# Residual of an attention and mixing kernel by DMA transposes, with a fused relu and residual, outputs one period later and pooled copies on ScalarE

## The chip, the cores and the metric

One core of one Trainium2 chip. The metric is the device time of one execution in microseconds (us); lower is better. A profile is of one execution; its span is about 1.7 us shorter than the time. Besides the time, each execution leaves its span and its mean granted TensorE clock.

## The reference

Attention over 8 batches, 8 heads, 576 positions, 64 per head, in two parts, then a mixing stage whose output this change touches:

```python
x   = attention(q_mean4, k_mean4, v_mean4).repeat(4) + attention(q, k, v, |i-j| < 4)   # -> (8, 576, 512)
theta = x @ w_theta
y   = w_tok_r @ (x * cos(theta)) + w_tok_i @ (x * sin(theta))    # over the 576 positions
u   = x + y
out = u + maximum(u @ w_ch, 0)
```

## The kernel before

It is a software pipeline over batches. In one period it runs attention of batch b+1 (generator `a`), the theta stage of batch b (`m`) and the mixing and output of batch b-1 (`x`). A string of slots sets the order in which the generators give their pieces; a scheduler may still move instructions. In the first period there is nothing to mix yet, and the slots of `x` transpose the token weights (`wt`).

```python
PERIOD = ("m a m a a x m a x m a a x m a x m a "
          "a a x a a x a a x a a x a a x a x a a x a x a a x").split()
# 13 slots of x; of wt in the first period
```

u is made transposed (channels on partitions: `uT`), because that is how the last matmul needs it. The output needs u with positions on partitions, so each of five output chunks transposes it back on TensorE:

```python
for c in range(5):                       # ... chunk 4 has 64 positions and is folded
    psr = w1(...)                        # PSUM, 4 buffers shared by all w1 tiles
    psx = w1(..., BF16)
    # 4 matmuls   psr += uT[:, dc, chunk].T @ wch[:, dc, :]
    # 4 transposes psx = uT[:, dc, chunk].T
    nc.scalar.activation(out=rel, in_=psr, func=AF.Relu)
    nc.vector.tensor_tensor(out=osb, in0=rel, in1=psx, op=ALU.add)
    nc.sync.dma_start(out=out[b, ...], in_=osb)
```

Attention turns q and k on TensorE (`pstr`) into PSUM; ScalarE copies the full part to `qT`, `kT`, VectorE the mean of four, "pooled", to `qdT`, `kdT`. The local attention's exponentials `pm` (ScalarE) are masked by two affine selects each on GpSimd (POOL), then multiplied with v (`psloc`):

```python
nc.scalar.copy(out=dst, in_=src)             # qT, kT
nc.vector.tensor_copy(out=dstd, in_=srcd)    # pooled copies, 8 a batch
# ...
nc.scalar.activation(out=pm, in_=psS, func=AF.Exp, scale=SCL)
nc.gpsimd.affine_select(out=pm, ...); nc.gpsimd.affine_select(out=pm, ...)
```

The softmax here doesn't subtract the row's maximum and nothing guards it: scores larger than these inputs give would overflow.

## Time and profile before

| | |
|---|---|
| time | 334.36 us median of 3 runs (333.44 to 340.42; 340.42 is over 1.5% above the fastest and counts as slow) |
| span of the profiled run, mean granted TensorE clock | 334.4 us, 0.923 of full |
| TensorE busy | 88% of the span |
| from the start to the first theta matmul (the head) | 39.9 us |
| first period | 36.1 us |
| the six periods after it, together | 216.8 us |
| from the last theta stage to the end (the tail) | 41.6 us |

Periods are counted from the first theta matmul (`psth`) of one batch to that of the next. The page gives 40 equal slices of 8.4 us; one digit is a busy share in tenths, and PEclk the granted TensorE clock in tenths, 9 also for full speed:

```profile
PE   1688898999996899979997899889998999699994
PEclk9995589558999999979999999999998999979999
```

PE is busy for most of the program, and the clock is at half in the middle of the head and of the first period (the digits 5). The record of the clock starts only with its first change, here at 20.5 us; the digits 9 before it are no measurement. A table of windows, cut at the theta stages, gives the same by stage. Its columns are the stretch and its length in us, the busy time (and count) of PE, its weight loads, VectorE, ScalarE and POOL, then the granted clock, the DMA share and GB/s. First period, last full period, tail:

```profile
39.92:75.98 36.06, 33.34 (x322) 23.67 (x319) 23.46 (x52) 22.75 (x33) 20.30 (x23) 0.69 0.97 198
...
255.94:292.80 36.86, 33.56 (x338) 22.63 (x340) 21.21 (x51) 23.33 (x34) 10.27 (x10) 0.95 0.10 34
292.80:334.40 41.60, 36.72 (x278) 25.58 (x280) 17.33 (x35) 11.41 (x20) 0.00 (x0) 0.96 0.18 61
```

### The profile page before, as it was taken

To read this page: it belongs to the slowest core of one execution; us is meant where nothing else is said; L and a number is where in the kernel's file an instruction comes from. 1 tells how busy PE (TensorE), PEld (TensorE's weight loads), DVE (VectorE), ACT (ScalarE), POOL (GpSimd) and SP (SyncE) were. 2 spreads that over 40 slices of the span, in tenths; PEclk is the share of its full clock that TensorE was granted. 3 is DMA by queue.
4 is the path that set the end of the run, shared out by engine and by line. 5 is a ranking of instruction groups with operands and counts; after the bars stand their busy time and mean duration, and the time that the engine had idled before them with its cause. 6 is when DMAs were issued, how large, how long until landed. Compare 5 with 4: busy or idle time off the path is not lost.

```text
span 334.4 us, 7314 instructions
## 1 busy us (share of the span) xinstructions
PE 294.0 (88%) x2940; PEld 204.9 (61%) x2954; DVE 195.0 (58%) x441; ACT 186.0 (56%) x280; POOL 159.2 (48%) x186
## 2 busy tenths in 40 slices
PE   1688898999996899979997899889998999699994
PEld 1664685576664676557664666566755766467672
DVE  5426846594546764685439664766466544934533
ACT  1264289424874668628872787377855596333302
POOL 6977504893049524964477447815790008300000
PEclk9995589558999999979999999999998999979999
DMA  8999999959302289639917895477012000300303
GB/s 221 235 321 218 234 285 228 200 92 201 77 2 90 62 142 206 143 104 204 194 38 212 153 209 101 142 176 142 2 65 78 2 0 14 117 16 2 136 7 141
DMA packets 107826, 43.57 MB, mean 130 GB/s; under 512 B 97424, under 2 KB 101520, under 8 KB 107792
## 3 DMA queue, kind: packets, MB, share of 16 engines
q1 hardware_dynamic: 107792, 43.10, 58.6%
q8 instruction: 23, 0.38, 0.5%
q14 instruction: 11, 0.09, 0.1%
HBM read 33.65 MB, written 9.44 MB: 129 GB/s over the span
## 4 chain that ended last, share of the span: by engine, by line
PE 39%; ACT 17%; POOL 13%; issue 12%; DVE 10%; DMA 5%; SPq 3%; POOLq 0%; DVEq 0%; ACTq 0%
PE psu L553 13%; PE psth L528 9%; POOL pm L414 4%; POOL pm L416 3%; DVE tmp L486 3%; DMA q<-in_q_dram 3%; ACT pd L367 3%; POOL k_tm L143 3%; PE psr L573 3%; PE pstr L314 2%; ACT pm L401 2%; DVE osb L600 2%; PE pstr L304 2%; PE psnd L428 2%; DVE x L493 2%
## 5 line engine op out<-in xcount | busy, mean ns | idle before, releaser
L553 PE MATMUL psu<-WT,z 120*128 120x288 bf16 (+1 forms) x640 | 92.3, 291 | 0.0
L553 PEld LDWEIGHTS <-z 120*128 120x128 bf16 (+1 forms) x640 | 60.3, 99 | 18.4 <-issue 0.2
L414 POOL TENSOR_SCALAR_AFFINE_SELECT pm<-pm 128x1024 bf16<-128x1024 bf16 (+1 forms) x32 | 33.4, 1052 | 56.0 <-ACT pm L401 52.9
L401 ACT ACTIVATE pm<-psS 128x1024 bf16<-128x1024 f32 (+1 forms) x40 | 38.6, 982 | 20.7 <-PE psS L393 18.7
L528 PE MATMUL psth<-wth,xT 128*120 128x512 bf16 (+1 forms) x160 | 45.1, 405 | 4.7 <-DVE xT L518 3.8
L598 ACT ACTIVATE rel<-psr 128x512 f32<-128x512 f32 (+1 forms) x40 | 22.4, 559 | 48.1 <-PE psr L573 38.6
L143 POOL CAST q_tm<-q 96x1024 bf16<-96x1024 f32 x18 | 22.6, 1276 | 46.4 <-PE pstr L314 21.0
L535 ACT ACTIVATE cs<-psth,pihc 120x512 bf16<-120x512 f32 (+1 forms) x40 | 27.5, 688 | 29.9 <-PE psth L528 29.8
L537 DVE TENSOR_TENSOR z<-cs,x 120x1024 bf16<-120x1024 bf16 (+1 forms) x40 | 32.5, 813 | 18.6 <-ACT cs L536 18.5
L562 DVE TENSOR_TENSOR uT<-psu,xT 128x288 bf16<-128x288 f32 x64 | 26.8, 452 | 28.0 <-PE psu L553 28.0
L325 ACT CAST qT<-pstr 128x576 bf16<-128x576 f32 x32 | 20.2, 642 | 36.7 <-PE pstr L314 21.3
L600 DVE TENSOR_TENSOR osb<-rel,psx 128x512 f32<-128x512 f32 (+1 forms) x40 | 25.2, 631 | 21.5 <-ACT rel L598 21.5
L416 POOL TENSOR_SCALAR_AFFINE_SELECT pm<-pm 128x1024 bf16<-128x1024 bf16 (+1 forms) x32 | 33.7, 1059 | 0.8
L573 PE MATMUL psr<-wch,uT 128*128 128x512 bf16 x114 | 31.2, 379 | 1.4 <-issue 0.9
L477 PEld LDWEIGHTS <-pm 128*128 128x128 bf16 (+1 forms) x320 | 16.5, 112 | 21.9 <-POOL pm L416 13.8
L528 PEld LDWEIGHTS <-xT 128*120 128x120 bf16 (+1 forms) x160 | 20.5, 139 | 14.1 <-DVE xT L518 4.8
L518 DVE COPY xT<-xTps 128x480 bf16<-128x480 bf16 (+1 forms) x40 | 15.5, 389 | 23.3 <-PE xTps L513 23.2
L477 PE MATMUL psloc<-v_w,pm 128*128 128x65 bf16 (+1 forms) x320 | 19.5, 209 | 9.3 <-POOL pm L416 5.7
L486 DVE TENSOR_TENSOR tmp<-psloc,rl 120x512 bf16<-120x512 f32 (+1 forms) x40 | 26.5, 683 | 0.0
L493 DVE TENSOR_TENSOR x<-tmp,psup 120x512 bf16<-120x512 bf16 (+1 forms) x40 | 26.4, 680 | 0.0
L143 POOL CAST k_tm<-k 96x1024 bf16<-96x1024 f32 x18 | 19.6, 1114 | 12.9 <-PE pstr L314 12.0
L536 ACT ACTIVATE cs<-psth 120x512 bf16<-120x512 f32 (+1 forms) x40 | 23.6, 590 | 0.0
(87 smaller groups left out, 457.1 us busy)
## 6 DMA issues: line engine op xcount, KB each, us to landing
v<-in_v_dram SPq DMA_DIRECT2D x32, 256.0 KB, 5.4
out_dram<-osb SPq DMA_DIRECT2D x32, 256.0 KB, 2.0
q<-in_q_dram SPq DMA_DIRECT2D x36, 192.0 KB, 4.0
k<-in_k_dram SPq DMA_DIRECT2D x36, 192.0 KB, 4.7
q<-in_q_dram SPq DMA_DIRECT2D x8, 288.0 KB, 5.1
k<-in_k_dram SPq DMA_DIRECT2D x8, 288.0 KB, 6.1
v<-in_v_dram SPq DMA_DIRECT2D x8, 200.0 KB
wt<-in_moe_w_tok_r_dram SPq DMA_DIRECT2D x4, 288.0 KB
```

What stands on the lines that cost most here:

```text
L143: eng(out=dst[:, c:c + 2], in_=src.rearrange("p (c h d) -> p c h d", c=NTR, d=D)[:, c:c + 2])
L401: nc.scalar.activation(out=pv, in_=ps[0:kw].rearrange("p e (j w) -> p (e j) w", w=P)[:, :, 0:qn], func=AF.Exp, scale=SCL,)
L414: nc.gpsimd.affine_select(out=pv, in_=pv, compare_op=ALU.is_ge, fill=0.0, base=off, pattern=[[0, 8], [-1, qn]], channel_multiplier=1)
L416: nc.gpsimd.affine_select(out=pv, in_=pv, compare_op=ALU.is_ge, fill=0.0, base=6 - off, pattern=[[0, 8], [1, qn]], channel_multiplier=-1)
L477: nc.tensor.matmul(out=pv[0:qn, par, j, :], lhsT=pms[c][0:kw, 4 * par + j, 0:qn], rhs=v_w[0:kw, c, 2 * j + par, 0:65], start=(j == 0), sto ...
L486: nc.vector.tensor_tensor(out=tmp[0:cnt].rearrange("p (j e d) -> p e j d", e=2, j=4), in0=pv[0:cnt, :, :, 0:D], in1=rl[0:cnt].unsqueeze(3) ...
L493: nc.vector.tensor_tensor(out=x[0:cnt], in0=tmp[0:cnt], in1=up[0:cnt], op=ALU.add)
L528: nc.tensor.matmul(out=th[0:cnt, :], lhsT=xT[:, dc, QS[c]:QS[c] + cnt], rhs=wth[:, dc, :], start=(dc == 0), stop=(dc == 3),)
L537: nc.vector.tensor_tensor(out=z[0:cnt, c, :, :], in0=cs[0:cnt], in1=xt[c][0:cnt].unsqueeze(1).to_broadcast([cnt, 2, DM]), op=ALU.mult,)
L553: nc.tensor.matmul(out=pss[hf][:, 0:288], lhsT=z[0:QC[c], c, ri, P * dc:P * dc + P], rhs=WT[0:QC[c], ri, c, 288 * hf:288 * hf + 288], star ...
L573: nc.tensor.matmul(out=psr, lhsT=uT[:, dc, P * c:P * c + P], rhs=wch[:, dc, :], start=(dc == 0), stop=(dc == 3),)
L600: nc.vector.tensor_tensor(out=osb[:, 0:w], in0=rel[:, 0:w], in1=psx[:, 0:w], op=ALU.add)
```

## The change

The intent: take the 20 transposes a batch off PE, and the relu off ScalarE. uT is copied by two DMA transposes a batch into `uX` (positions on partitions), and one VectorE operation computes max(psr, 0) + uX. To give the transposes time, outputs come one period later, as a fourth generator `o`. ScalarE, freed of the relu, takes the pooled copies.

```diff
-    # relu on ScalarE, 4 (5) x 4 PE transposes, add on VectorE
-    nc.scalar.activation(out=rel[:, 0:w], in_=psr[:, 0:w], func=AF.Relu)
-    nc.vector.tensor_tensor(out=osb[:, 0:w], in0=rel[:, 0:w], in1=psx[:, 0:w], op=ALU.add)
+    # in mix, after every second dc:
+    nc.vector.tensor_copy(out=uT[:, dc - 1:dc + 1, S:640], in_=uT[:, dc - 1:dc + 1, 512:S])
+    nc.sync.dma_start_transpose(out=uX[:, dc - 1:dc + 1]..., in_=uT[:, dc - 1:dc + 1, :]...)
+    # in output, a period later:
+    nc.vector.scalar_tensor_tensor(out=osb, in0=psr, scalar=0.0, in1=uX[lo:hi, e:e + n, c, :],
+                                   op0=ALU.max, op1=ALU.add)
...
-                nc.vector.tensor_copy(out=dstd, in_=srcd)
+                (nc.vector.tensor_copy if b < WIDE else nc.scalar.copy)(out=dstd, in_=srcd)
...
-        "m a m a a x m a x m a a x m a x m a "
-        "a a x a a x a a x a a x a a x a x a a x a x a a x"
+        "m a m a a x m a x m a a x m a x m a x "
+        "a a o a a o a a o a a a a a o a x a a x a x a o"
...
-    for b in range(B + 1):
+    for b in range(B + 2):
+        run(a=attention(b + 1) ..., m=modulate(b) ...,
+            x=wt if b == 0 else mix(b - 1) if b <= B else None, o=output(b - 2) if b >= 2 else None)
...
-    t = moep.tile([P, S], FP32, tag=("osb", "rel")[ct % 2], bufs=3, ...)   # weight tiles, 6 buffers
+    t = moep.tile([P, S], FP32, tag="osb", bufs=4, ...)                    # 4 buffers
```

More of the change, by code (lines that the diff above doesn't have):

```diff
@@ L168, in staircase @@
                                     base=base, pattern=[[sgn * step, cols]], channel_multiplier=sgn * mul)
-    pw = moep.tile([TR, NTR, SD], BF16, tag="rel", bufs=3, name="pw")
+    pw = moep.tile([TR, NTR, SD], BF16, tag="pw", bufs=1, name="pw")
     nc.vector.memset(pw, 0.25)
@@ L241, in build_WT @@
     def build_WT():
-        w_tm = [moep.tile([P, 5, S], BF16, tag="uT", name=f"wtm{ri}") for ri in range(2)]
+        w_tm = [moep.tile([P, 5, S], BF16, tag="uX", name=f"wtm{ri}") for ri in range(2)]
         pieces = []
@@ L245, in build_WT @@
             for ct in range(5):
-                t = moep.tile([P, S], FP32, tag=("osb", "rel")[ct % 2], bufs=3, name=f"wt32_{ri}{ct}")
+                t = moep.tile([P, S], FP32, tag="osb", bufs=4, name=f"wt32_{ri}{ct}")
                 rows = OC[ct]
@@ L273, in build_WT @@
                 yield
+    uTs = [wpool.tile([P, 4, 640], BF16, name=f"uT{i}") for i in range(2)]
     xs = {}
@@ L500 @@
     state = {}
+    mixed = {}
     def modulate(b):
@@ L546, in mix @@
         xT, z = state.pop(b)
-        uT = moep.tile([P, 4, S], BF16, tag="uT", name=f"uT{b}")
+        uT = uTs[b % 2]
+        uX = moep.tile([P, 4, 5, P], BF16, tag="uX", name=f"uX{b}")
+        mixed[b] = (uT, uX)
         for dc in range(4):
@@ L565, in mix, with output @@
                 )
+            if dc % 2:
+                nc.vector.tensor_copy(out=uT[:, dc - 1:dc + 1, S:640], in_=uT[:, dc - 1:dc + 1, 512:S])
+                nc.sync.dma_start_transpose(
+                    out=uX[:, dc - 1:dc + 1].rearrange("p e c d -> p (e c) d"),
+                    in_=uT[:, dc - 1:dc + 1, :].rearrange("p e t -> p (e t)"),
+                )
             yield
+    def output(b):
+        uT, uX = mixed.pop(b)
         for c in range(5):
             psr = w1(f"psr{c}_{b}")
-            psx = w1(f"psx{c}_{b}", BF16)
+            osb = moep.tile([P, DM], FP32, tag="osb", bufs=4, name=f"osb{c}_{b}")
             if c < 4:
-                w = DM
                 for dc in range(4):
@@ L576, in mix @@
                     )
-                for dc in range(4):
-                    nc.tensor.transpose(
-                        out=psx[:, P * dc:P * dc + P], in_=uT[:, dc, P * c:P * c + P], identity=ident,
-                    )
+                parts = [(0, P, 0, 4)]
             else:
-                w = DM // 2
                 for dc in range(4):
@@ L586, in mix @@
                         nc.tensor.matmul(
-                            out=psr[64 * hf:64 * hf + 64, 0:w], lhsT=uT[:, dc, 512:576],
-                            rhs=wch[:, dc, w * hf:w * hf + w],
+                            out=psr[64 * hf:64 * hf + 64, 0:256], lhsT=uT[:, dc, 512:576],
+                            rhs=wch[:, dc, 256 * hf:256 * hf + 256],
                             start=(dc == 0), stop=(dc == 3),
                         )
-                for j in range(2):
-                    for hf in range(2):
-                        nc.tensor.transpose(
-                            out=psx[64 * hf:64 * hf + 64, P * j:P * j + P],
-                            in_=uT[:, 2 * hf + j, 512:576], identity=ident,
-                        )
@@ L597, in mix @@
-            rel = moep.tile([P, DM], FP32, tag="rel", bufs=3, name=f"rel{c}_{b}")
-            nc.scalar.activation(out=rel[:, 0:w], in_=psr[:, 0:w], func=AF.Relu)
-            osb = moep.tile([P, DM], FP32, tag="osb", bufs=3, name=f"osb{c}_{b}")
-            nc.vector.tensor_tensor(out=osb[:, 0:w], in0=rel[:, 0:w], in1=psx[:, 0:w], op=ALU.add)
-            if c < 4:
-                nc.sync.dma_start(out=out[b, P * c:P * c + P, :], in_=osb)
-            else:
-                for hf in range(2):
-                    nc.sync.dma_start(out=out[b, 512:576, w * hf:w * hf + w], in_=osb[64 * hf:64 * hf + 64, 0:w])
+                parts = [(0, 64, 0, 2), (64, 128, 2, 2)]
@@ L606, in mix @@
+            for lo, hi, e, n in parts:
+                nc.vector.scalar_tensor_tensor(
+                    out=osb[lo:hi, 0:P * n].rearrange("p (e d) -> p e d", d=P),
+                    in0=psr[lo:hi, 0:P * n].rearrange("p (e d) -> p e d", d=P),
+                    scalar=0.0, in1=uX[lo:hi, e:e + n, c, :], op0=ALU.max, op1=ALU.add,
+                )
+                nc.sync.dma_start(out=out[b, P * c:P * c + hi - lo, P * e:P * e + P * n], in_=osb[lo:hi, 0:P * n])
             yield
     PERIOD = (
-        "m a m a a x m a x m a a x m a x m a "
@@ L612, with run @@
-        "a a x a a x a a x a a x a a x a x a a x a x a a x"
+        "m a m a a x m a x m a a x m a x m a x "
+        "a a o a a o a a o a a a a a o a x a a x a x a o"
     ).split()
-    def run(a, m, x):
-        gens = {"a": a, "m": m, "x": x}
+    def run(**gens):
         for s in PERIOD:
-            g = gens[s]
-            if g is not None:
-                next(g, 0)
-        for s in ("m", "x", "a"):
+            if gens[s] is not None:
+                next(gens[s], 0)
+        for s in "mxoa":
@@ L627 @@
     next(wt)
-    for b in range(B + 1):
-        run(attention(b + 1) if b + 1 < B else None,
-            modulate(b) if b < B else None,
-            mix(b - 1) if b >= 1 else wt)
+    for b in range(B + 2):
+        run(a=attention(b + 1) if b + 1 < B else None,
+            m=modulate(b) if b < B else None,
+            x=wt if b == 0 else mix(b - 1) if b <= B else None,
+            o=output(b - 2) if b >= 2 else None)
 _INS = ['q', 'k', 'v', 'moe_w_theta', 'moe_w_tok_r', 'moe_w_tok_i', 'moe_w_ch']
```

## The prediction

> **What bounds the kernel now.** I read the page's busy shares first, then the table of windows cut at the first theta matmul (psth) of each batch, then the timeline of one period engine by engine, and last the tail. The program is a software pipeline: in one period it modulates batch b, mixes b-1 and runs attention on b+1.
>
> ```profile
> PE 294.0 (88%) x2940; PEld 204.9 (61%) x2954; DVE 195.0 (58%) x441; ACT 186.0 (56%) x280; POOL 159.2 (48%) x186
> ...
> core 0: us, PE busy (x) PEld busy (x) DVE busy (x) ACT busy (x) POOL busy (x), PEclk, DMA share, GB/s
> ...
> 149.69:185.11 35.42, 32.40 (x349) 22.11 (x351) 21.81 (x52) 24.02 (x37) 19.75 (x19) 0.99 0.79 158
> 185.11:220.75 35.64, 32.46 (x350) 22.37 (x352) 22.56 (x51) 23.41 (x36) 20.10 (x19) 1.00 0.78 158
> 220.75:255.94 35.19, 32.68 (x350) 22.45 (x352) 22.45 (x51) 23.41 (x36) 20.44 (x19) 1.00 0.37 88
> ```
>
> Periods are all 35.2 to 35.7 us, whether the DMA share is 0.79 or 0.37, so loads don't set them. PE looks 92% busy, but its ends are modelled. From start to start in the timeline, one psth or psr matmul costs 0.86/4 = 0.215 us of issue, one psu 1.47/12 = 0.1225, six pstr 0.32, eight psS or psloc 0.32. By that measure a period has about 30.6 us of PE issue and 4.9 us of gaps. PE is the fullest engine, not a saturated one. The rest is in the second half of the period:
>
> ```profile
> 238.83 1.02 ACT L401 ACTIVATE pm<-psS 128x1024 bf16<-128x1024 f32 x1
> ...
> 239.93 1.09 POOL L414 TENSOR_SCALAR_AFFINE_SELECT pm<-pm 128x1024 bf16<-128x1024 bf16 x1 [1.91 <-ACT pm L401]
> 241.09 1.09 POOL L416 TENSOR_SCALAR_AFFINE_SELECT pm<-pm 128x1024 bf16<-128x1024 bf16 x1
> 242.22 1.09 POOL L414 TENSOR_SCALAR_AFFINE_SELECT pm<-pm 128x1024 bf16<-128x1024 bf16 x1
> 243.38 1.09 POOL L416 TENSOR_SCALAR_AFFINE_SELECT pm<-pm 128x1024 bf16<-128x1024 bf16 x1
> 244.43 2.14 POOL L414 TENSOR_SCALAR_AFFINE_SELECT pm<-pm 128x1024 bf16<-128x1024 bf16 x2
> 246.52 2.14 POOL L416 TENSOR_SCALAR_AFFINE_SELECT pm<-pm 128x1024 bf16<-128x1024 bf16 x2
> 248.61 0.88 POOL L414 TENSOR_SCALAR_AFFINE_SELECT pm<-pm 100x768 bf16<-100x768 bf16 x1
> 249.56 0.88 POOL L416 TENSOR_SCALAR_AFFINE_SELECT pm<-pm 100x768 bf16<-100x768 bf16 x1
> ```
>
> From the first exp on, POOL masks without a gap for 10.5 us; the last local matmul waits for the last mask, and the next period starts 5.5 us later. POOL at 48% of the span is full in exactly this stretch. The end of the program is different, PE issues back to back:
>
> ```profile
> 324.66 1.03 PE L573 MATMUL psr<-wch,uT 128*128 128x512 bf16 x3
> 325.52 0.39 PE L578 MATMUL psx<-ident,uT 128*128 128x128 bf16 x4
> 325.75 1.03 PE L573 MATMUL psr<-wch,uT 128*128 128x512 bf16 x4
> 326.61 0.39 PE L578 MATMUL psx<-ident,uT 128*128 128x128 bf16 x4
> ```
>
> Here the start-to-start spacing tells what the removed transposes are worth: psx to the next psr is 325.75 - 325.52 = 0.23 us for four, though the group shows 0.39 us busy.
>
> [...] The trace has the first at 219 ns each, pipelined to 0.06; it holds no transposing DMA. [...] the 256 KB writes of this kernel land in 2.0 us, so I take 3 to 5 us from issue to landing. [...] the trace's residual adds take 684, so I leave the fused operation, still one pass with a PSUM input, at 0.69. [...] the trace's ScalarE copies of 128x144 take 279. [...]
>
> **The change, part by part.**
> 1. PE loses 4 x 4 + 4 transposes a batch: 5 x about 0.22 = 1.1 us a period, 8.8 us in all. This is the most that the PE part alone can give, 2.6%; the group's busy time (20 x 0.219 = 4.4 us) would promise four times that.
> 2. ACT loses the relu, 4 x 0.60 + 0.38 = 2.8 us a period, in the second half. It gains 8 pooled copies x 0.28 = 2.2 us in the first half, where from the theta stage to the first exp it already works about 15 of 18 us.
> 3. DVE loses the 8 pooled copies (8 x 0.30 = 2.4 us). The fused operation replaces the add one for one, except that the last chunk becomes two (+0.4), and two small copies of the tail columns come in (about 0.15 each, my guess). The residual no longer waits for the relu; PSUM is freed sooner.
> 4. The order changes. In the built program, PE has three output chunks (12 psr) but only 52 instead of 63 psu matmuls before the first scores: +12 x 0.215 - 11 x 0.1225 = +1.3 us, plus one or two pstr groups (0.3) that used to come before the theta stage. Hence the first exp comes about 1.4 us later. Going down ACT's new order with the trace's durations (five sine pairs at 1.28, copies at 0.64 + 0.28, table load 1.28, pooled exps 2.35) gives the same: first mask at about +20 to +20.6 after the theta start, against +19.2 now.
> 5. From there POOL's 10.5 us stand, and its built order has two or three casts of the next k and v inside this stretch (1.03 each; now zero to three), so +2.1 to 3.1. After the last mask the path to the next theta stage is shorter: no relu, no residual of this batch in the way, and the copy of x's first transposed chunk now stands ahead of the last tmp on DVE. I work it out as 0.6 (psloc) + 0.5 (psr, pstr) + 0.2 + 0.2 (transposes) + 0.4 (copy) + signals, 2.3 us against 3.5 to 5.5.
> 6. A middle period: 20.3 + 10.5 + 2.6 + 2.3 = 35.7, give or take one, against 35.5. So four middle periods give nothing. The second batch's period (37.95 now, four casts in the mask stretch) should lose about 2.5 us, having no output chunks and three casts; that with no casts (36.86 now) about 2.5 too.
> 7. The tail. Outputs of two batches follow the last mix instead of one, but their PE time has only moved there, and output 6 is used as filler. What is new: after the last mix come the second uT add (0.4), copy (0.15), the DMA transpose (3 to 5), then four fused operations and two half ones, 4 x 0.69 + 2 x 0.41 = 3.6 us. The last osb now ends 6 us after the last mix (324.7 to 330.7); then about 9 us. With about 3.9 us more psr after the last theta start and 1.5 us fewer PE transposes and gaps in it, the tail gets 4 to 6 us longer; I take 5.
> 8. The head: weight tiles have 4 buffers instead of 6, so SyncE stands at the fifth and the tenth weight load until POOL has cast the first of each half, and the loads of k for the third batch move from 45 to about 62 us. They are cast at 70 anyway. I put +0.5.
> Sum: -2.5 - 2.5 + 0.5 (middle periods, rounded) + 5 + 0.5 = +1 us, 335.4. My stage estimates lean cautious (the gaps of PE should shrink when its partners wait less), so I move to 333.
>
> **Rivals.**
> A: PE is the bound all through. Then 8.8 us go, and some of the 4.9 us gaps in each period with them: 334 - 9 - 6 x 1 + 5 = 324. For it: 92% in the windows. Against: the unbroken POOL stretch and the later first exp.
> B: the DMA transpose is slow[...]. Then SyncE's order (second transpose, then the next q loads) delays every load[...]. [...] Nothing in the profile before shows such a DMA, so I can't exclude it.
> C: ACT becomes the bound of the first half by the copies: the first exp another 1 us later in six periods, 340.
> D: POOL waits for k or v inside the mask stretch since q loads now stand behind the second transpose. The period from 113.95 had q loads at +4.6 us and k casts at +14.5 without harm, and I expect loads no later than that unless B holds.
>
> **Range and chances.** Between A (324) and the sum with C (341), with a tail of the range for B: 321 to 347, prediction 333. Faster by over 2% (under 327.7) needs periods below about 34 us with POOL's 10.5 us standing: 0.28. Slower by over 2% (above 341) needs B or C with D: 0.24. Within 2%: 0.48.
>
> **What would show it.** Right: no psx and no relu; period starts 35 to 36 us apart; first mask at +20 or later; POOL's masks with casts in between and no gaps; under 3 us from last mask to next theta start; transposes landing in 3 to 5 us; the last fused operation about 9 us after the last psu. Wrong in A's favour: periods near 33.5 and PE gaps gone. Wrong in B's: transposes of 8 us or more, SyncE standing still, q or k casts waiting for DMA. Wrong in C's: ACT without idle time before the first exp and PE waiting for its copies.

The forecast's sum came to +1 us, 335.4, and was shaded to 333. The 3 to 5 us for the transposing DMA, part of step 7's +5, is the estimate, above the 2.0 us in which the 256 KB writes of the kernel before land. In the paragraph of trace figures "the first" is a 128x128 transpose on TensorE. The 0.15 us for a small copy was a guess; the trace after has 0.18.

## The result and the profile after

350.16 us median of 4 runs (347.53 to 352.18) against 334.44 us for the kernel before on the same chip. The ratio is 1.047 (95% interval 1.040 to 1.055): slower. Ratios here compare fast runs of the same rounds and are not quite the ratio of the medians.

```profile
PE 292.7 (85%) x2794; PEld 196.9 (57%) x2794; DVE 199.7 (58%) x417; ACT 175.1 (51%) x288; POOL 154.6 (45%) x186
...
PE   0777995899979799879995999799968997799991
PEclk9995598556985999989999899999999999899996
```

146 PE matmul records fewer (2940 to 2794; 160 transposes were taken out, and the trace before lacks 14 of its 192 psr), yet PE's busy time fell by 1.3 us only. In the clock row the half-clock stretch of the first period reaches further (5, 5, 6 at the eighth to tenth digit, before 5, 5, 8), and a new one appears in the second period (8, 5 at the twelfth and thirteenth). By stage:

```profile
39.67:81.03 41.36, 35.84 (x341) 26.55 (x339) 25.10 (x52) 24.83 (x39) 23.54 (x27) 0.67 0.87 182
81.03:117.51 36.48, 31.41 (x285) 20.78 (x282) 16.21 (x36) 19.28 (x33) 16.87 (x18) 0.81 0.39 75
...
264.00:298.92 34.92, 30.05 (x307) 19.37 (x304) 20.28 (x45) 21.11 (x33) 10.20 (x10) 1.00 0.19 52
298.92:345.80 46.88, 39.12 (x264) 25.07 (x264) 21.97 (x47) 5.86 (x10) 0.00 (x0) 0.91 0.39 109
```

| stage, us | before | after | difference | predicted |
|---|---|---|---|---|
| head | 39.92 | 39.67 | -0.25 | in the next |
| first period | 36.06 | 41.36 | +5.30 | +0.5 |
| second period | 37.97 | 36.48 | -1.49 | -2.5 |
| four middle periods | 141.99 | 146.49 | +4.50 | +0.5 |
| last full period | 36.86 | 34.92 | -1.94 | -2.5 |
| tail | 41.60 | 46.88 | +5.28 | +5 |
| span | 334.40 | 345.80 | +11.40 | +1 |

This is the fastest of the four runs of the kernel after; the mean span of the four is 348.3 us.

**The first period.** The timeline of SyncE's issues shows a stand of 14 us, and that of PE the weight transposes (wps) at the period's end:

```profile
46.73 0.42 SPq L255 DMA_DIRECT2D w<-in_moe_w_ch_dram  x1
61.28 0.48 SPq L248 DMA_DIRECT2D wt<-in_moe_w_tok_i_dram  x1
61.82 5.54 SPq L94 DMA_DIRECT2D k<-in_k_dram  x6
```

```profile
70.48 1.67 PE L267 MATMUL wps<-ident,wtm 128*120 128x128 bf16 x10
...
78.78 0.85 PE L267 MATMUL wps<-ident,wtm 128*96 128x128 bf16 x5
...
81.03 1.91 PE L532 MATMUL psth<-wth,xT 128*120 128x512 bf16 x4
```

In the kernel before 20 of these 50 transposes ran at 52.9 to 55.9 us, between the pooled scores and at full clock; here all run from 62.7 us on and at half clock (ten in 1.67 us; at full clock, in run 15 below, ten take 1.11). The stand and the late transposes come together here but are not one cause: run 5 below has the old slots with four buffers, and SyncE stands there too (46.5 to 61.4 us), yet 20 transposes run at 52.4 to 55.4 us and the first period takes 37.5 us.

**The middle.** Two period starts of this same run, one after a sparse stretch and one after a denser one. Windows of 3.4 us, with the clock third from last:

```profile
186.60:190.00 3.40, 1.70 (x23) 1.10 (x23) 2.27 (x6) 0.00 (x0) 3.40 (x5) 1.00 0.00 0
190.00:193.40 3.40, 3.40 (x27) 2.44 (x25) 2.67 (x6) 2.92 (x5) 0.15 (x1) 0.55 0.51 96
...
223.20:226.60 3.40, 2.22 (x30) 1.54 (x29) 3.04 (x8) 0.28 (x1) 2.99 (x4) 1.00 0.00 0
226.60:230.00 3.40, 3.38 (x33) 2.66 (x34) 2.65 (x6) 3.37 (x6) 0.00 (x0) 1.00 0.69 136
```

And PE's timeline there:

```profile
188.66 0.55 PE L480 MATMUL psloc<-v_w,pm 100*96 100x65 bf16 x8 [1.70 <-POOL pm L419]
...
190.58 1.96 PE L532 MATMUL psth<-wth,xT 128*120 128x512 bf16 x4
...
226.62 1.07 PE L532 MATMUL psth<-wth,xT 128*120 128x512 bf16 x4 [0.18 <-DVE xT L522]
```

PE waits 1.70 us for the last mask, is busy for 1.70 of 3.40 us, and in the next 3.4 us its clock is half: the four theta matmuls take 1.96 instead of 1.07 us, at the start of the next period. (The lengths of two such periods are not compared here: some q transposes fall now before, now after the theta stage, which moves work between neighbours.) Taken in windows of 1 us over the whole trace, the clock is always 0.50 or 1.00 but for transitions, and its half-clock stretches last 3.4 us or multiples (3.4, 10.2, 17.1, 27.3), but for one that the end of the program cuts. In the profile of the kernel before they sum to 51 us, in that of the kernel after to 70. The full-clock stretches between them are whole multiples of 3.41 us too (13.7 to 105.8 us), so in both traces all changes of the clock lie on one grid of 3.41 us, the clock's own steps in what follows. The two windows shown above do not start with the clock's own steps; in those, PE is busy for 1.70 us from 186.9 to 190.3, and for 2.25 and 2.92 us from 221.0 to 224.4 and on to 227.8.

**The tail.** VectorE's timeline:

```profile
333.43 0.82 DVE L568 TENSOR_TENSOR uT<-psu,xT 128x288 bf16<-128x288 f32 x2 [1.63 <-PE psu L559]
...
334.50 0.18 DVE L573 COPY uT<-uT 128x128 bf16<-128x128 bf16 x1
...
338.79 2.48 DVE L603 SCALAR_TENSOR_TENSOR osb<-psr,uX 128x512 f32<-128x512 f32 x4 [3.65 <-DMA uX<-uT]
341.68 0.88 DVE L603 SCALAR_TENSOR_TENSOR osb<-psr,uX 64x256 f32<-64x256 f32 x2 [0.41 <-DMA out_dram<-osb]
```

From the last uT add to the last osb it takes 9.1 us (333.43 to 342.56); before, 6.0. 3.65 us of it is VectorE standing for the transposing DMA, which lands in 3.9 us at the median (3.4 to 4.5; SyncE takes 1.26 to 1.37 us to issue one, up to 3.27 among loads):

```profile
uX<-uT SPq DMA_TRANSPOSE x16, 3.9
```

### The profile page after: what moved, and what is told of

It reads as the page before. It is cut to its first block, busy times and chain, and to the rows that moved or that the text cites. A ratio compares the mean times of both kernels' runs of the same rounds, so it can differ in the third digit from the quotient of the medians.

```text
span 345.8 us, 7013 instructions
## 1 busy us (share of the span) xinstructions
PE 292.7 (85%) x2794; PEld 196.9 (57%) x2794; DVE 199.7 (58%) x417; ACT 175.1 (51%) x288; POOL 154.6 (45%) x186
## 4 chain that ended last, share of the span: by engine, by line
PE 49%; POOL 17%; ACT 13%; DVE 9%; issue 6%; DMA 4%; SPq 1%; DVEq 0%; ACTq 0%; POOLq 0%
PE psu L559 17%; PE psth L532 11%; POOL pm L417 8%; POOL pm L419 6%; PE pstr L317 5%; PE psr L587 3%; ACT pd L370 2%; ACT L370 2%; ACT vd L350 2%; DMA q<-in_q_dram 2%; ACT pm L404 2%; PE xTps L517 2%; PE pstr L307 2%; POOL k_tm L143 2%; DVE tmp L489 2%
## 5 line engine op out<-in xcount | busy, mean ns | idle before, releaser
L559 PE MATMUL psu<-WT,z 120*128 120x288 bf16 (+1 forms) x640 | 96.6, 294 | 0.8 <-DVE uT L568 0.4
L328 ACT CAST qT<-pstr 128x576 bf16<-128x576 f32 x32 | 20.7, 646 | 73.5 <-PE pstr L317 57.1
L541 DVE TENSOR_TENSOR z<-cs,x 120x1024 bf16<-120x1024 bf16 (+1 forms) x40 | 31.8, 794 | 20.0 <-ACT cs L540 19.8
L603 DVE SCALAR_TENSOR_TENSOR osb<-psr,uX 128x512 f32<-128x512 f32 (+1 forms) x48 | 28.6, 600 | 24.9 <-PE psr L587 20.5
L143 POOL CAST q_tm<-q 96x1024 bf16<-96x1024 f32 x18 | 20.2, 1126 | 45.7 <-DMA q<-in_q_dram 24.2
L587 PE MATMUL psr<-wch,uT 128*128 128x512 bf16 x128 | 32.6, 380 | 0.0
L480 PE MATMUL psloc<-v_w,pm 128*128 128x65 bf16 (+1 forms) x320 | 20.4, 212 | 14.2 <-POOL pm L419 12.0
L489 DVE TENSOR_TENSOR tmp<-psloc,rl 120x512 bf16<-120x512 f32 (+1 forms) x40 | 27.3, 684 | 0.3
L496 DVE TENSOR_TENSOR x<-tmp,psup 120x512 bf16<-120x512 bf16 (+1 forms) x40 | 26.6, 668 | 0.1
L143 POOL CAST k_tm<-k 96x1024 bf16<-96x1024 f32 x18 | 18.7, 1043 | 7.2 <-DMA k<-in_k_dram 4.0
L470 PE MATMUL psup<-xd,ru 72*128 72x512 bf16 (+1 forms) x48 | 20.1, 458 | 0.9 <-DVE x L496 0.8
```

The lines of the kernel that those rows point to most:

```text
L143: eng(out=dst[:, c:c + 2], in_=src.rearrange("p (c h d) -> p c h d", c=NTR, d=D)[:, c:c + 2])
L480: nc.tensor.matmul(out=pv[0:qn, par, j, :], lhsT=pms[c][0:kw, 4 * par + j, 0:qn], rhs=v_w[0:kw, c, 2 * j + par, 0:65], start=(j == 0), sto ...
L489: nc.vector.tensor_tensor(out=tmp[0:cnt].rearrange("p (j e d) -> p e j d", e=2, j=4), in0=pv[0:cnt, :, :, 0:D], in1=rl[0:cnt].unsqueeze(3) ...
L541: nc.vector.tensor_tensor(out=z[0:cnt, c, :, :], in0=cs[0:cnt], in1=xt[c][0:cnt].unsqueeze(1).to_broadcast([cnt, 2, DM]), op=ALU.mult,)
L559: nc.tensor.matmul(out=pss[hf][:, 0:288], lhsT=z[0:QC[c], c, ri, P * dc:P * dc + P], rhs=WT[0:QC[c], ri, c, 288 * hf:288 * hf + 288], star ...
L587: nc.tensor.matmul(out=psr, lhsT=uT[:, dc, P * c:P * c + P], rhs=wch[:, dc, :], start=(dc == 0), stop=(dc == 3),)
```

## The experiments

Theory at the start: the loss is the first period (weights drained late), the tail (DMA latency) and a middle set by POOL. Rivals: the transposing DMAs hold up the loads; the ScalarE copies delay the scores; the clock. Eighteen runs, each in 3 rounds beside the kernel before on the same chip. All runs of the changed kernels were fast except three of the fourth. "Half" is the time at half clock: 2 x (1 - mean clock) x span, averaged over the fast runs, without the time before the clock's record starts (about 20 us); the stages are those of the one profiled run, in us.

| run | median | before | head | first | six periods | tail | half |
|---|---|---|---|---|---|---|---|
| kernel before | | 334.44 | 39.92 | 36.06 | 216.82 | 41.60 | 48 |
| kernel after | 350.16 | 334.44 | 39.67 | 41.36 | 217.89 | 46.88 | 75 |
| 1 first period as before | 350.23 | 335.84 | 40.89 | 37.35 | 224.28 | 48.18 | 76 |
| 2 last residual on PE | 346.22 | 335.84 | 39.93 | 41.18 | 220.74 | 44.65 | 69 |
| 3 no transposes, zeroed tile | 346.97 | 335.84 | 43.68 | 40.67 | 216.42 | 43.53 | 49 (see text) |
| 4 pooled copies on VectorE | 353.12 | 335.84 | 39.95 | 39.38 | 219.77 | 46.90 | 67 (1 run) |
| 5 outputs not a period later | 362.44 | 334.80 | 40.32 | 37.54 | 238.04 | 44.50 | 89 |
| 6 all residuals on PE | 350.36 | 334.80 | 39.23 | 41.17 | 222.53 | 45.87 | 75 |
| 7 after, 4 fills | 346.70 | 334.80 | 39.75 | 39.13 | 220.78 | 45.24 | 41 |
| 8 before, 4 fills | 339.45 | 334.80 | 39.09 | 36.79 | 220.83 | 39.99 | 28 |
| 9 slots as before | 347.34 | 335.69 | 41.26 | 39.71 | 217.15 | 46.88 | 81 |
| 10 before, ScalarE copies | 342.45 | 335.69 | 40.06 | 38.09 | 219.92 | 41.63 | 61 |
| 11 run 1 with 4 fills | 344.56 | 335.69 | 40.50 | 37.01 | 219.88 | 45.21 | 40 |
| 12 runs 1 and 2, 2 fills | 343.17 | 335.69 | 39.76 | 36.59 | 219.48 | 44.47 | 41 |
| 13 order alone | 349.63 | 334.85 | 39.90 | 38.68 | 223.87 | 45.85 | 67 |
| 14 no transposes, clean | 348.26 | 334.85 | 40.16 | 41.20 | 220.44 | 43.50 | 75 |
| 15 run 10 with 2 fills | 330.77 | 334.85 | 38.94 | 36.56 | 212.78 | 39.92 | 28 |
| 16 before, 2 fills at the last group | 334.85 | 334.85 | 40.31 | 35.60 | 214.98 | 41.61 | 45 |
| 17 before, 2 fills | 333.03 | 334.98 | 39.76 | 36.04 | 215.35 | 39.95 | 28 |
| 18 run 15 with one-row fills | 343.04 | 334.98 | 39.82 | 41.74 | 218.42 | 39.92 | 52 |

**1. The first period as before** (e1_head6)

```diff
-        for s in PERIOD:
+        for s in PERIOD0 if gens["x"] is wt else PERIOD:     # PERIOD0: the old string
-    t = moep.tile([P, S], FP32, tag="osb", bufs=4, ...)
+    t = moep.tile([P, S], FP32, tag=("osb", "wtb")[ct % 2], bufs=(4, 2)[ct % 2], ...)
```

> The kernel after, with the first period as before: the weight builder gets its 13 early slots again (the old slot string for that period alone) and six weight buffers instead of four. Head theory (the first period is 5.5 us longer because the 20 weight transposes ran at its end, at half the TensorE clock, after a load that waited for POOL's cast): the first period falls from 41.4 to 36-37 us, the whole from 350 to about 345. Rival (a disturbance that the transposing DMAs or the later outputs cause): there is neither in the first period, so it predicts nothing here, and the first period stays near 41.

The first period fell to 37.35 us as the theory had it. The whole did not move: 350.23. In the profiles (the slowest of this kernel's four runs against the fastest of the kernel after's) the periods after it took 6.4 us more, with more of them at half clock. So the slots and buffers together are behind the first period (run 5 parts them: it is the slots), but a gain there did not reach the end. That made the clock the main suspect.

**2. The last batch's residual on PE** (e2_tail)

```diff
-            if dc % 2:
+            if dc % 2 and not (b == B - 1):
+            pe = b == B - 1      # then 20 PE transposes, ACT relu, DVE add as in the kernel before
```

> The kernel after, with only the last batch's residual by 20 PE transposes, ACT relu and DVE add, as before; all other batches keep their DMA transposes. Tail theory (5.3 us of the loss: the last uT, its copy, a transposing DMA of about 4 us, then fused operations at 0.69 us each): the last stretch falls from 46.9 to 42-43 us, the whole from 350 to about 346. Rival (the tail is longer because two batches' outputs follow the last mix, whatever way the residual takes): it stays at 46 or more.

346.22, and the tail 44.65: 2.2 of the tail's 5.3 us are the transposing DMA and what follows it, the other 3 stay. By count these are the further output that now follows the last theta stage: 16 psr matmuls of 512 columns (0.215 us each) and 8 of 256 (0.46 us for all, from 329.10 to 329.56 us in the kernel before) are 3.9 us, less the 20 transposes that are saved there (1.1 us).

**3. and 14. No transposing DMAs** (e3_notranspose, e14_notranspose_clean)

```diff
-        uX = moep.tile([P, 4, 5, P], BF16, tag="uX", name=f"uX{b}")
+        uX = uX0                                              # run 3: one tile of zeros
+        uX = uT.rearrange("p e (c d) -> p e c d", d=P)        # run 14: the untransposed uT
-                nc.sync.dma_start_transpose(...)
```

> Wrong on purpose: the kernel after without its 16 transposing DMAs; the residual is read from one constant tile of zeros, everything else (small copies, fused operation, order) stays. Mask-stretch theory (the middle periods are set by when POOL's mask stretch starts and by the casts in it): the six middle periods stay within 0.5 us of the kernel after (about 36.5 on average) and only the tail loses 3-4 us; the whole about 346. Rival, contention (the transposing DMAs hold up the queue, so q, k and v come late and POOL waits): the middle periods fall by 1-2 us each and the whole to about 338.

> Wrong on purpose: the kernel after without its transposing DMAs; the fused operation reads the untransposed uT where it read the transposed copy, so there is no zeroing any more. If the transposing DMAs cost nothing but the tail: head 39.7, middle periods as in the kernel after, tail 43.5, the whole 346-347. If they also delay the loads and so bring casts into the mask stretch and the clock down: middle periods near 35, half-clock time 50-60, the whole 340-343.

Both give wrong results. Run 3 has an artefact: its head is 43.7 instead of 39.7 us. The zeroing delays the first PE instruction by 0.9 us only; but PE stays slow through the whole head (the first four theta matmuls take 1.91 us at 43.68), and the clock's record starts at 45.8 us instead of 19.6. So its 49 us leave out more than the others' and are not to be compared. Run 14 has none and gives 348.26, a tail of 43.50 instead of 46.88, a first period and half-clock time as in the kernel after. It misses its 346 to 347: the whole fell by 1.9 us only, as the six periods took 2.5 us more in its profile. So the transposing DMAs cost the tail about 3.4 us, and taking them out makes nothing else shorter; contention is out.

**4. Pooled copies on VectorE again** (e4_dvecopies)

```diff
-                (nc.vector.tensor_copy if b < WIDE else nc.scalar.copy)(out=dstd, in_=srcd)
+                nc.vector.tensor_copy(out=dstd, in_=srcd)
```

> The kernel after, with the pooled copies on VectorE again. If the copies on ScalarE delay the first exp (8 x 0.28 us in ScalarE's filled first half, the rival C of the prediction): the first mask comes 1 to 1.5 us sooner after the theta start in each middle period, periods fall by about 1 us, the whole to 343-345. If the three early output chunks on PE delay the scores instead: the first mask stays at about +20.7 and the whole within 1.5 us of 350.

Three of four runs counted as slow (over 1.5% above the fastest, 347.77); it is no gain. From the third period on the first masks came at +20.5 to +22.1 us: no better. The first period of the one fast run is 39.38 us against 41.36, though.

**5. Outputs in the same period** (e5_samelag)

```diff
+    def both(b):
+        yield from mix(b)
+        yield from output(b)
-            x=wt if b == 0 else mix(b - 1) ..., o=output(b - 2) if b >= 2 else None)
+            x=wt if b == 0 else both(b - 1), o=None)          # and the old slot string
```

> The kernel after with its order taken back: outputs follow their own mix in the same period, in the slot string of the kernel before; the DMA transposes, the fused operation and the copies on ScalarE stay. Order theory (the loss comes from the outputs moved one period later: a first period that drains the weight transposes at its end, a mask stretch left without dense matmuls so that the TensorE clock is halved more often, a tail with two batches' outputs): half-clock time, 69 us in the kernel after, returns to about 50 as before, first period 36, tail 44-45, the whole 333-338. Rival (the transposing DMAs, the fused operation or the copies cost the time themselves): it stays at 345 or more.

362.44: the expectation of the order theory fell flat. With no period between, VectorE stands for the transposes in the middle of the program too. The waits of this run:

```profile
DVE osb L607 <- DMA uX<-uT: 11.6, 5, 3.6
```

The columns are us in all, times, longest. 11.6 us of direct waits are not the whole of 28 us; in the second period (47.8 us) GpSimd waited 9.3 us for one exponential, and half-clock time rose to 89 us. How these waits chain up was not followed further. The delay of a period is needed by the DMA transposes, so they cannot be tried without it.

**6. and 13. The order without DMA transposes** (e6_pe_residual, e13_order_alone)

```diff
+            pe = True            # run 6: every residual by PE transposes, relu, add
+                nc.vector.tensor_copy(out=dstd, in_=srcd)     # run 13: and the pooled copies on VectorE
```

> The kernel after with its order and its ScalarE copies, but every residual by 20 PE transposes, ACT relu and DVE add; no DMA transposes. Order theory: first period still 41 us, half-clock time still 65-75 us, tail 44-45 (as in the run with only the last batch so), the whole 345-350. Rival (DMA transposes delay the loads and with them the periods): the middle periods return to 35.5 and the whole to about 340.

> The order alone: outputs one period later in the new slots, four weight buffers; but residuals by PE transposes, ACT relu, DVE add, and pooled copies on VectorE, as before. If the order is what thins PE in the mask stretch: half-clock time 70 us or more, first period 40-41, tail 45, the whole 346-350. If the ScalarE copies were needed for the loss (350.4 with both, 342.5 with the copies alone): about 341-343.

350.36 and 349.63 (the first period of run 13 is 38.7 us, not 40 to 41). Outputs one period later in the new slots cost 15 us by themselves; with the ScalarE copies on top it is the same, and with the DMA transposes on top (the kernel after, 350.16) again the same. What the DMA transposes and the fused operation save on PE and ScalarE does not show. So the order is enough for a loss of this size. It is not the same loss, stage by stage: the six periods of run 13 are 6 us longer than those of the kernel after, its first period 2.7 us shorter. "Order" here is the later outputs, the new slots and the four weight buffers together.

**7. and 8. Useless work** (e7_fill_after, e8_fill_before)

```diff
             ps = w2(f"psloc{c}_{b}")
+            for i in range(4 if b > 0 else 0):
+                nc.tensor.matmul(out=ps[:, 1, :], lhsT=wth[:, 0, 0:P], rhs=wth[:, 0, :], start=True, stop=True)
```

> The kernel after with useless work added: four 128x512 matmuls (4 x 0.215 us) before each psloc group of the batches from the second on, into the PSUM tile that psloc then overwrites; 140 matmuls, about 30 us of PE time in all. Clock theory (PE too sparse in the mask stretch, so the clock is halved in steps of 3.4 us there and at the start of the next period): half-clock time falls from 69 us to about 45, first masks come at +19.5 instead of +20.9 after the theta start, and the whole falls to 342-347 although PE has more to do. Rival (PE is the bound): the whole rises by up to 30 us, to 365-380; neither: 350.

> The kernel before with the same useless matmuls. Clock theory: its half-clock windows at 58-79, 146-151 and 256-260 us (27 us in all) mostly go, in the first period above all; 330-336 against 335, since its second halves are denser and the fill then also costs some time. Rival (PE bound): 350 or more.

140 more matmuls of 128x512 made the kernel after 3.5 us faster (ratio 1.037, 1.031 to 1.043, against 1.047, 1.040 to 1.055), and half-clock time fell from 75 to 41 us. PE is not the bound; its clock matters. (From the third period on first masks came at +19.85 to +20.5, not quite +19.5.) The kernel before lost 4.7 us by the same fill (ratio 1.014): it was dense already. The pair also shows what is left where the clock is nearly even (in the six periods, one stretch of 10 us at half clock against none): six periods 220.78 against 220.83, first period +2.3, tail +5.2. The prediction's claim is about the four middle periods: these take 148.4 against 147.3 us, 1.1 us more, with no half clock in either. But the fill itself makes the kernel before's middle 5.3 us longer, so this is not a test of the bare kernels.

**9. The old slots for the mixing** (e9_old_slots)

```diff
-        "m a m a a x m a x m a a x m a x m a x a a o a a o a a o a a a a a o a x a a x a x a o"
+        "m a m a a x m a x m a a x m a x m a a a x a a x a a x a a x a a o a o a a o a o a a o"
```

> The kernel after with another slot string: the mixing keeps all its slots of the kernel before (the scheduler builds 60 to 63 psu and no psr ahead of the scores, as before), and the output chunks, still one period later, stand in the mask stretch, where they stood before. Clock theory: PE is dense in the mask stretch again, half-clock time falls from 69 us to 50-60, middle periods to 35-35.5, the whole to 340-345 (the tail stays at 46, the first period at 38-41). Rival (the middle lost its time to the later scores of PE's new order): the first masks come at +19.2 whatever the clock does, and the periods fall likewise; told apart by the half-clock windows at the periods' starts. If neither: 350.

347.34, and half-clock time did not fall (81 us): the expectation fails. Moving the output chunks back into the mask stretch does not by itself keep the clock; with all the mixing ahead of the scores the stretch has 4 psr a chunk and still no transposes.

**10. One part alone: the ScalarE copies** (e10_before_act_copies)

```diff
-                nc.vector.tensor_copy(out=dstd, in_=srcd)                  # in the kernel before
+                (nc.vector.tensor_copy if b < WIDE else nc.scalar.copy)(out=dstd, in_=srcd)
```

> The kernel before with one part of the change alone: the eight pooled copies on ScalarE instead of VectorE. Rival C of the prediction (ScalarE bounds the first half): first masks 1 us or more later than +19.2 and the whole 340-342. If ScalarE has room between the sines: first masks within 0.4 us of +19.2, the whole 333-337.

342.45 (ratio 1.021, 1.014 to 1.027), the size of rival C. But its reason is wrong: the first masks came at +18.7 in the last three periods, sooner than +19.2, and these periods took 34.4 to 35.4 us. What grew are the first four, by 8.0 us together (153.2 against 145.2). The scheduler now puts all four q transposes ahead of the theta stage, where PE waits for ScalarE's copies, at half clock. PE's timeline at the end of the first period:

```profile
73.50 0.26 PE L314 MATMUL pstr<-ip,q_tm 96*128 96x120 bf16 x1 [0.36 <-ACT qdT L326]
...
78.09 0.26 PE L314 MATMUL pstr<-ip,k_tm 96*128 96x120 bf16 x1 [0.71 <-ACT qdT L326]
78.15 1.91 PE L528 MATMUL psth<-wth,xT 128*120 128x512 bf16 x4
```

**11. and 12. Causes taken away together** (e11_head_fill, e12_all_three)

```diff
# 11: edits of runs 1 and 7.   12: edits of runs 1 and 2, and the fill with range(2 ...)
```

> The kernel after with the first period of run one (old slots, six weight buffers) and the useless matmuls of the fill run together. If the 4 us that the old first period gained were lost again to the clock, then with the clock held they stay: 342-343 against 346.7 for the fill alone, first period 36-37. Rival (the weights' transposes only move, and the loads set the sum of the first periods): 346-347.

> The kernel after with the old first period, the last batch's residual by PE transposes, and half the fill (two useless matmuls before each psloc group): the three causes taken away together. If they are the whole of the loss and add up: first period 36-37, periods 35-36, tail 42-44, half-clock time about 45, the whole 335-339, level with the kernel before. If something else costs the time: above 342.

Run 11: 344.56 against 346.70 for the fill alone. With the clock held, 2.1 of the first period's gain stay, half of what was expected. Run 12 misses: 343.17 instead of 335 to 339. The tail is still 2.9 us longer than before and the periods 2.7 us; with half the fill the clock still fell twice in the two periods after the first, whose first half no fill reaches. The three causes do not add up to the whole. The amount of half clock is not all that is left, either: it is 41 us here, less than the 48 of the kernel before, and the run is still 7.5 us slower.

**15. and 17. The fill where the order is the old one** (e15_act_copies_fill, e17_before_fill2)

```diff
# 15: run 10 and the fill with range(2 ...)      17: the kernel before and the fill with range(2 ...)
```

> The kernel before with the ScalarE copies and two useless matmuls ahead of each psloc group. Its undisturbed periods were 34.4 to 35.4 us, but 58 us ran at half clock. If holding the clock is all that it lacks: half-clock time 35-40, periods 35-36 throughout, the whole 332-336 against 342.5 without the fill. If the copies cost time by themselves: 339 or more.

> The kernel before with two useless matmuls ahead of each psloc group, the copies still on VectorE. If the ScalarE copies are worth something once the clock is held: 334-336, 4 us above the same fill with the copies on ScalarE (330.8). If the fill alone made that gain: 330-332.

Run 15 is faster than both kernels: 330.77, ratio 0.988 (0.979 to 0.996), outputs correct; at the 2% that a verdict asks for it stays unclear. The same ScalarE copies that cost 7 us alone no longer cost time with the fill: run 15 is 2.3 us below run 17 (333.03, ratio 0.994, 0.991 to 0.998). That gain is less than the 4 us expected and not secure, as the two come from different chips and the intervals overlap.

**16. Very little fill** (e16_before_fill_last)

```diff
+            for i in range(2 if b > 0 and c == 4 else 0):     # in the kernel before
```

> The kernel before with only two useless matmuls a period, ahead of the last psloc group. Clock theory: the three half-clock windows at the starts of periods (10 us, worth about 0.35 us each us by the slope among runs of one kernel) go for 0.2 us a period: 332-334 against 335. If two are too few: 335-336.

334.85, ratio 0.997 (0.991 to 1.004): too few. Half-clock time fell by 4 us only.

**18. The same order, fills that hardly work** (e18_one_row_fill)

```diff
-    nc.tensor.matmul(out=ps[:, 1, :],   lhsT=wth[:, 0, 0:P],   rhs=wth[:, 0, :],   start=True, stop=True)
+    nc.tensor.matmul(out=ps[0:1, 1, :], lhsT=wth[0:1, 0, 0:1], rhs=wth[0:1, 0, :], start=True, stop=True)
```

> The kernel of the run with ScalarE copies and fill, instruction for instruction in the same order on every engine, but each useless matmul multiplies one row by one column of weights (still 512 wide), so PE is occupied as long and hardly works. If the other order made the gain, or if the clock follows PE's occupied time: 331 and 28 us at half clock, as there. If the clock follows the work done in the array: half-clock time 55-60 and 340-343, and then the order is not the cause.

A fill makes the scheduler place some other groups differently, so runs 7 to 17 alone leave open whether the clock or the order made the gain. Run 18 has the instructions of run 15 in the same order on every engine; only the fills use one row and one column of the array. 343.04 against 330.77, half-clock time 52 against 28. PE's timeline and the windows of run 15, first:

```profile
64.22 1.04 PE L475 MATMUL psloc<-wth 128*128 128x512 bf16 x2
```

```profile
66.00:70.00 4.00, 3.79 (x36) 2.19 (x37) 3.52 (x8) 0.00 (x0) 4.00 (x6) 0.78 1.21 197
70.00:74.00 4.00, 3.53 (x46) 2.80 (x45) 3.96 (x10) 2.20 (x6) 3.65 (x5) 1.00 0.49 110
...
78.00:82.00 4.00, 4.00 (x37) 2.91 (x34) 2.74 (x6) 2.23 (x5) 0.00 (x0) 1.00 0.93 193
```

and run 18:

```profile
64.57 1.01 PE L475 MATMUL psloc<-wth 1*1 1x512 bf16 x2
```

```profile
66.00:70.00 4.00, 4.00 (x28) 1.58 (x26) 2.98 (x8) 0.00 (x0) 3.93 (x7) 0.50 1.21 199
70.00:74.00 4.00, 4.00 (x26) 1.80 (x25) 2.36 (x7) 0.00 (x0) 4.00 (x5) 0.50 0.37 68
...
78.00:82.00 4.00, 3.29 (x29) 2.73 (x27) 1.59 (x4) 2.17 (x5) 1.34 (x2) 0.50 1.30 217
```

The fills themselves take as long in both (two in 1.04 and 1.01 us); around each pair PE loses about 0.18 us more with one row, as the gaps between starts show. With the array filled the clock is back at 1.00 from about 68 us; with one row it stays at 0.50 to the end of the first period, though PE is busy 4.00 of 4.00 us. Order does not make these 12 us. Most of them go with the clock: in the profiles 11.7 us, of which 8.4 lie in the first two periods, where run 18 has most of its extra half clock, but 1.7 in the last four full periods, at full clock in both, and 0.9 in the head, ahead of any fill. In this pair the clock goes with the work done in the array (28 us at half clock with it filled, 52 with one row), not with PE's occupied time.

**A rule that the traces give.** Which work the clock follows can be counted in the 20 traces, the two kernels' and the runs'. Cut each into the clock's own steps of 3.41 us and add up each step's matmuls as rows x columns x moving columns, in units of one full matmul (128 x 128 weights, 512 columns), transposes included; a matmul that lies across a border is split by time. Under about 5.5 units the next step is at half clock, above it at full clock: right in 1860 of 1875 steps, whichever clock the step itself had. No limit on PE's busy time does better than 1616, and without the transposes none does better than 1715. (The traces of the two kernels alone: 185 of 186 steps at a limit of 5.5; 160 at best by busy time, 175 without the transposes.) A limit read from the kernel after alone (5.4) is right in 1764 of the 1780 steps of the other 19 kernels. The step from 186.9 us above had 4.6 units, those from 221.0 and 224.4 had 6.1 and 8.8; the step from 77.7, where PE transposes weights at half clock and is busy for 3.40 of 3.40 us, has 5.4 and does not bring the clock back.

**How much of it is the clock.** Among the 72 fast runs of kernels with at least two (each taken against its own kernel's mean), the span grows by 0.35 us for each us at half clock (correlation 0.71). The kernel after has 26.6 us more of it than the kernel before (74.9 in 4 runs, 48.3 in 33). By that slope this is about 9 us of the 14.7 between the mean spans (348.3 and 333.6); an estimate, since a slope among runs is no experiment, and run 12 warns that less half clock alone does not bring the time back. The rest, 5 to 6 us, is the size of the tail.

## Why the prediction was wrong

It said 333 us with 0.24 for slower by over 2%. The result is 5% slower, outside the range. The profile lies 10.4 us above the sum of its steps: 4.8 in the first period, 4.0 in the four middle periods, 1.6 in the second and the last; the tail held.

- **Step 8, the head and first period (+0.5), failed**: +5.3. It saw SyncE's stand and the loads moved to 62 us, and this happened to the us. But it looked for the cost in the loads and the buffers only. It did not look at what the shorter slot string does in the first period, where `x` is the weight builder: 8 slots instead of 13, and all 50 transposes from 62.7 us on, at half clock. Run 1 takes 4.0 us of it back, and run 5, with the old slots and the four buffers, 3.8: the slots, not the buffers. The copies on ScalarE, for which it put down nothing here, go with another 2.0 to 2.5 us (run 10 over the kernel before 2.0, run 4 under the kernel after 2.0, run 13 under run 6 2.5; one profile each).
- **Steps 4 and 6, the middle periods ("35.7, give or take one ... give nothing"), failed in two terms and lacked a third**: 36.6 on average against 35.5 before, +4.5 us for the four instead of +0.5. The first mask came at +20.7, +20.9, +21.9 and +20.9, 21.1 on average against the 20.3 of the sum; the mask stretch took 12.6 us against 13.1, with two or three casts in it as foreseen; from the last mask to the next theta stage it was 2.0 to 4.4 us, 2.9 on average against 2.3. That is +0.8 - 0.5 + 0.6 a period. The term that it lacked is the granted clock: it multiplied counts by full-clock durations throughout ("one psth or psr matmul costs 0.215 us") and had the clock column of its own windows table before it. The clock shows in the third of these periods: it starts with 3.1 us at half clock and has the mask at +21.9. But it is not the whole: the four hold 6.7 us at half clock against 3.4 before, which as lost PE time is under 2 us of the 4.5, and in two of them the first masks came at +20.7 and +20.9 although no half clock lies before them. There the new order (12 psr ahead of the scores, as step 4 saw) is the likely cause, mis-sized: the first scores (psS) came at +19.2 and +19.3 there against +17.5 on average before, 1.7 us later where step 4 had about 1.4 (its own sum, 1.23 + 0.3, is 1.5).
- **Step 1, PE loses 1.1 us a period, brought no gain that shows.** "PE is the fullest engine, not a saturated one" was the right reading; its consequence, a slower clock for a PE with less work between waits (here 4.6 units in the step from 186.9 us, and the next at half clock), was not drawn. By the count above the transposes taken out are 4.5 units of work a period. Whether it is they that thin the stretch is not shown: run 6, which puts them back in the new order, had as much half clock (75 us) and was no faster, so the order thins it enough alone.
- **Step 7, the tail (+4 to +6, taken 5), held**: +5.28. From the last uT add to the last osb 9.1 us ("about 9"), the transpose 3.9 us ("3 to 5"), the fused operation 0.69 us. Run 2 gives 2.2 of it to the DMA path, run 14 3.4; the extra output is the rest.
- **Step 6, second and last period (-2.5 each)**: -1.5 and -1.9. The second spent 13.7 us at half clock, 10.2 of them from 101.6 us on, in the mask stretch, which has no output chunks to fill it.
- **The shading from 335.4 to 333** ("the gaps of PE should shrink") had no number behind it and went the wrong way.
- **Rivals.** A (PE bound, 324) is refuted by run 7. B (slow DMA transpose) is refuted by 3.4 to 4.5 us from issue to landing. C has about the right size alone (run 10) with a wrong mechanism: the copies cost the first four periods, by transposes that wait for them, and not a later first exp in all six. D did not happen: the q casts waited 24 us for loads in all, but POOL's mask stretch has no gap in any period. None of the four was the clock or the first period's slots.

What stays open: which part of the order (the later outputs or the new slots) costs the middle; why the new order thins PE enough by itself although run 9, which puts psr back into the mask stretch, did not help; and a control like run 18 for the kernel after, whose gain by fill (run 7) came with a changed order.

## What to carry to other kernels

Before pricing a change on a kernel whose PE is not saturated, read the granted clock by stage and ask whether the change leaves the array less work (counted per step of the clock, not as busy time: right in 1860 steps here against at most 1616) in a stretch where it waits. Here a step with 4.6 units of work was followed by one at half clock, in which four theta matmuls took 1.96 us instead of 1.07, and the kernel after, with 20 transposes a batch fewer, had 26.6 us more at half clock than the kernel before (run 6, with the transposes back in the new order, had as much). A slot string or buffer count that serves the steady state also serves the first and last rounds, where other work runs in the same slots; price these separately. When single parts each cost much and together no more, look for a state that they share, and hold it fixed (here by useless matmuls) before comparing parts.
